# Output weights of attention B loaded at a later gate: the first piece of q of the fifth chunk in place of the fourth piece of q of the third

## The chip, the cores and the metric

The kernel runs on one core of a Trainium2 chip. The metric is the device time of one execution in microseconds; the median of several runs is compared. The core has a matmul engine (TensorE, PE in the profile, PEld for its weight loads), VectorE (DVE), ScalarE (ACT), GpSimd (POOL) and SyncE (SP). SyncE issues nearly all transfers between DRAM and on-chip memory, in order, on one hardware queue that sixteen DMA engines serve.

## The reference, cut to what matters

Two attentions over 2048 positions of width 640, with 32 heads of 20, side by side in the output. All inputs are bf16.

```python
def _A_ref(x, wq, wk, wv, wo, beta):            # 4 segments of 512
    for s in range(N):
        logits = einsum('bhqd,bhkd->bhqk', qs, ks) * scale + mask      # causal in the segment
        a_dot  = einsum('bhqk,bhkd->bhqd', softmax(logits), vs)
        a_mem  = (phi(qs) @ M) / (phi(qs) @ z + 1e-06)                 # memory of earlier segments
        o      = g * a_mem + (1.0 - g) * a_dot                         # g = sigmoid(beta)
        M, z   = M + phi(ks)^T vs, z + sum(phi(ks))
    return o @ wo
def _B_ref(x, wqkv, wo):                        # causal, window of 256
    o = softmax(masked(q k^T * Dh ** -0.5)) v
    return o @ wo
return concatenate([A, B], axis=-1)
```

## The kernel before

The work is cut into eight chunks of 512 positions that alternate between the two attentions: A0, B0, A1, B1, A2, B2, A3, B3. In the code they are numbered from 0, so the "third chunk" is number 2 (A1) and the "fifth" is number 4 (A2). Each chunk passes through these stages: q and k projected in five pieces of 128 columns (`qk_job`, result copied from PSUM by VectorE at line 557), v projected in two halves of four tiles (`v_job`; the copy to vA at line 733 multiplies by 1 − g), scores in batches (line 814), their exponential on ScalarE (line 830), masks on GpSimd (line 869) and VectorE (line 847), probabilities times v (line 883, line 904 in the last chunk), a transpose and a normalisation (lines 949 to 1000), and the output projection with wo (`final_job`, copied out at line 1099).

Some data must change partitions between stages, and that goes through transfers on SyncE's queue. Three of the eight head groups of q and k are stored to a scratch in DRAM (line 509) and read back in another layout (line 517); phi(q) and phi(k) go the same way (lines 619, 626, 651, 646). In the A chunks, once the first half of v is written to vA, two transfers copy the lower 64 rows of vA to a tile vS (line 757); the second half of v, which writes the same tile vA, may be written only after the first of these copies has read it. In the B chunks the tiles vL, vU and vX are filled alike (line 783). Outputs go through a scratch and a transposing transfer (lines 1021 and 1040) before the projection. The inputs x of later chunks are loaded in three pieces when their buffer comes free (line 355).

The order of TensorE's work is written out by hand in the string `PLAN`. The kernel is emitted once by a planner, `Flow`, that keeps an estimated time for each engine and for the DMA queue. It decides at which point of the emitted program a transfer is issued, and with that the order on SyncE's queue, which is then fixed. The weights wait in a list `self.loads`; each has a gate (a time that is known only when some earlier piece of work has been emitted) and a due time counted from the gate. The front of the list is issued when its gate is known and either the planned queue is idle or the due time has come:

```python
        t = max(self.sp - 100.0, self.fabric - BACK)
        gate, _, due = self.loads[0]
        if gate:
            if gate() is None:
                return None
            return min(max(t, gate() - 400.0), gate() + due)
```

`load_w` adds a weight tile of [128, 2, 5, 320] as two transfers of 400 KB, one for each half of its columns (line 319), each into a tile of its own that nothing else uses. The tile wo_B serves the output projections of B0, B1, B2 and most of B3. A third load, wo_end, stands behind it in the list with a gate in the last chunk.

In the emitted program each transfer of SyncE takes the next of eight completion semaphores in turn, and does not start before the transfer eight places earlier has landed.

Of the kernel before, what the change touches and what calls it, by code (L numbers as in the profile page):

```python
# [267 lines left out]
class _K:  # L268
# [1034 lines left out]
    def body(self, xA, A_wq, A_wk, A_wv, A_wo, A_beta, xB, B_wqkv, B_wo, out2d):  # L1303
# [65 lines left out]
                                   None, 22000.0)  # L1369
        wo = {}  # L1370
        wo["A"] = self.load_w("wo_A", A_wo, self.known(0, "scored"), 6000.0)
        wo["B"] = self.load_w("wo_B", B_wo[0], self.known(2, "q", 3), 6000.0)

        wo["end"] = self.load_w("wo_end", B_wo[1], self.known(NC - 1, "q", KT - 1), 9000.0,
                                self.wt["wk_A"][:].rearrange("p m k c -> p (m k c)").rearrange(
# [336 lines left out]
```

## Time and profile before

| what | value |
|---|---|
| runs | 332.38, 332.24, 330.19 us; median 332.24 |
| profiled execution | 332.54 us, its span 330.7 us |
| granted clock of TensorE | 1.000 |
| TensorE, ScalarE, GpSimd, VectorE busy | 96%, 91%, 80%, 77% of the span |
| transfers | 47.45 MB, mean 143 GB/s |
| wo_B issued by SyncE | from 73.17 us, 2 transfers |
| first matmul that reads wo_B | 149.6 us |

Busy time of TensorE is modelled from the instructions, so 96% does not say that it runs at its peak. In the rows quoted below, a time in brackets at the end of a timeline row is how long the engine stood still before it, with what ended that. "SPq" rows are the issuing of transfers by SyncE, not the movement of data. In the table of waits the three numbers are total microseconds, number of times and the longest.

### The profile page before, as it was taken

Reading aid. Unit: us, or ns where it says so; the run is one execution under the profiler, and the core shown is the slowest. Engines: PE = TensorE matmul, PEld = TensorE weight load, DVE = VectorE, ACT = ScalarE, POOL = GpSimd, SP = SyncE. Lnnn points to the kernel's source line nnn. Section 1 sums busy time; section 2 is a strip of 40 time slices with the busy share of each in tenths; the row PEclk is TensorE's granted clock in tenths of the full one; section 3 lists DMA queues with packets and bytes.
Section 4 is the critical chain, followed back from the end, with each engine's and each line's share of the span. In section 5 each row is a group of like instructions: output and inputs, shape, how many; then the busy total and the mean of one; then the engine's idle time right before and its main releaser. Section 6 shows DMA issues by size and latency. Waiting matters only on the chain.

```text
span 330.7 us, 16968 instructions
## 1 busy us (share of the span) xinstructions
PE 316.4 (96%) x7195; PEld 176.2 (53%) x7195; DVE 255.8 (77%) x533; ACT 299.6 (91%) x333; POOL 265.4 (80%) x672
## 2 busy tenths in 40 slices
PE   7999999998999999999999999999999999999984
PEld 2454546555445455646653546456654445666652
DVE  6777767797977787999867897988777798876753
ACT  1979999998999998989999999899999999979962
POOL 8466679997759899976886999998975899989850
PEclk9999999999999999999999999999999999999999
DMA  7975945675589354165689146117868027397642
GB/s 210 388 250 135 194 138 108 150 193 159 135 214 217 67 115 132 22 141 147 138 216 174 33 86 157 50 32 154 147 181 186 14 54 185 107 233 159 109 127 80
DMA packets 76266, 47.45 MB, mean 143 GB/s; under 512 B 48382, under 2 KB 73182, under 8 KB 76190
## 3 DMA queue, kind: packets, MB, share of 16 engines
q1 hardware_dynamic: 75469, 45.71, 57.7%
q8 instruction: 56, 0.92, 1.2%
q10 hardware_dynamic: 720, 0.66, 0.7%
q14 instruction: 21, 0.16, 0.2%
HBM read 17.62 MB, written 16.96 MB: 105 GB/s over the span
## 4 chain that ended last, share of the span: by engine, by line
PE 36%; DVE 5%; ACT 3%; DMA 2%; POOL 2%; issue 1%; SPq 1%; ACTq 0%; DVEq 0%
PE m L935 19%; PE sc L814 7%; PE m L883 5%; ACT pt L830 3%; PE m L930 2%; DVE tt L949 2%; PE m L904 1%; DMA xT<-scr_o 1%; DVE pt L847 1%; DMA scr_o<-o 1%; POOL pt L869 1%; DVE kA L557 1%; POOL o L987 1%; DVE ot L1099 0%; PE m L686 0%
## 5 line engine op out<-in xcount | busy, mean ns | idle before, releaser
L830 ACT ACTIVATE pt<-sc 128x1024 bf16<-128x1024 f32 (+2 forms) x306 | 282.9, 1026 | 15.1 <-PE sc L814 12.9
L869 POOL TENSOR_SCALAR_AFFINE_SELECT pt<-pt 128x128 bf16<-128x128 bf16 (+1 forms) x512 | 178.0, 376 | 49.8 <-ACT pt L830 42.8
L949 DVE STREAM_TRANSPOSE tt<-m 128x512 f32<-128x512 f32 x88 | 61.2, 709 | 24.7 <-PE m L883 15.9
L987 POOL TENSOR_TENSOR o<-tt,rr 128x320 bf16<-128x320 f32 x64 | 48.5, 758 | 4.7 <-DVE rr L977 3.9
L814 PE MATMUL sc<-qB,kB 20*64 20x64 bf16 (+2 forms) x1728 | 39.9, 217 | 0.8 <-ACT pt L830 0.3
L935 PEld LDWEIGHTS <-xT 128*128 128x128 bf16 x296 | 26.7, 97 | 18.4 <-issue 6.1
L847 DVE TENSOR_TENSOR pt<-pt,ends 128x1024 bf16<-128x1024 bf16 (+2 forms) x50 | 36.4, 739 | 0.0
L1099 DVE CAST ot<-m 128x320 bf16<-128x320 f32 x58 | 28.1, 486 | 9.8 <-PE m L935 8.4
L814 PEld LDWEIGHTS <-kB 20*64 20x64 bf16 (+1 forms) x1728 | 22.2, 98 | 22.4 <-issue 20.5
L814 PE MATMUL sc<-qA,kA 20*64 20x64 bf16 (+4 forms) x1024 | 33.5, 237 | 0.5 <-ACT pt L830 0.4
L935 PEld LDWEIGHTS <-oT 128*128 128x128 bf16 x244 | 21.5, 97 | 12.5 <-issue 3.3
L814 PEld LDWEIGHTS <-kA 20*128 20x128 bf16 (+1 forms) x1024 | 13.4, 97 | 22.4 <-issue 21.3
L935 PE MATMUL m<-wBv,xT 128*128 128x320 bf16 x147 | 24.2, 299 | 0.9 <-DVE tt L949 0.4
L883 PE MATMUL m<-pt,vA 128*32 128x192 bf16 (+3 forms) x512 | 23.6, 274 | 0.2
L935 PE MATMUL m<-wo_A,oT 128*128 128x320 bf16 x125 | 21.0, 300 | 0.8 <-DVE kA L557 0.8
L935 PE MATMUL m<-xT,wBq 128*128 128x512 bf16 x82 | 21.4, 380 | 0.3 <-DVE tt L949 0.3
L935 PE MATMUL m<-xT,wBk 128*128 128x512 bf16 x81 | 20.7, 381 | 0.0
L935 PE MATMUL m<-wv_A,xT 128*128 128x320 bf16 x119 | 20.0, 300 | 0.2 <-DVE vA L733 0.2
L738 DVE CAST vB<-m 128x320 bf16<-128x320 f32 x32 | 15.6, 488 | 5.4 <-PE m L935 3.1
L935 PE MATMUL m<-wo_B,oT 128*128 128x320 bf16 x109 | 18.6, 300 | 0.8 <-DVE tt L949 0.4
L557 DVE CAST qB<-m 128x512 bf16<-128x512 f32 x20 | 13.8, 688 | 6.7 <-PE m L930 3.4
L935 PE MATMUL m<-xT,wk_A 128*128 128x512 bf16 x69 | 17.7, 379 | 1.2 <-DMA xT<-in_A_x_dram 1.1
(127 smaller groups left out, 460.2 us busy)
## 6 DMA issues: line engine op xcount, KB each, us to landing
out_dram<-ot SPq DMA_DIRECT2D x29, 160.0 KB
scr_o<-o SPq DMA_DIRECT2D x28, 160.0 KB
xT<-in_B_x_dram SPq DMA_DIRECT2D x8, 288.0 KB
xT<-in_A_x_dram SPq DMA_DIRECT2D x8, 256.0 KB
scr_pk<-e SPq DMA_DIRECT2D x15, 128.0 KB
vS<-vA SPq DMA_DIRECT2D x16, 87.0 KB
vL<-vB SPq DMA_DIRECT2D x8, 174.0 KB
scr_kA<-kA SPq DMA_DIRECT2D x16, 60.0 KB
```

Source lines behind the costliest of these rows:

```text
L557: nc.vector.tensor_copy(out=dst[:, m, at:at + L], in_=ps[:, :])
L738: nc.vector.tensor_copy(out=dst, in_=src)
L814: nc.tensor.matmul(ps[j // 2][h0:h1, j % 2, c0:c0 + nq], lhsT=k[rows, g, k0:k0 + h1 - h0], rhs=q[rows, g, q0:q0 + nq], start=True, stop=Tr ...
L830: nc.scalar.activation(out=pt[:, :, lo:hi], in_=ps[i][:, :, lo:hi], func=ACT.Exp, scale=self.scale)
L847: nc.vector.tensor_tensor(out=blk, in0=blk, in1=self.ends[:, c0, :].unsqueeze(1).unsqueeze(1) .to_broadcast([P, 2, n // SH, SH]), op=ALU.mult)
L869: nc.gpsimd.affine_select(out=blk, in_=blk, pattern=pat, compare_op=ALU.is_ge, fill=self.zero, base=base, channel_multiplier=mul)
L883: nc.tensor.matmul(O[HD * j:HD * j + HD, q0:q0 + nq], lhsT=v[:, at_head(h):at_head(h) + HD], rhs=pts[j // 2][:, j % 2, c0:c0 + nq], start= ...
L930: self.nc.tensor.matmul(ps[s, 0:n], lhsT=lhsT[:, s], rhs=rhs, start=start, stop=stop, tile_position=(0, HD * j), skip_group_check=True)
L935: self.nc.tensor.matmul(ps[:, 0:n], lhsT=lhsT, rhs=rhs, start=start, stop=stop, skip_group_check=True)
L949: self.nc.vector.transpose(out=tt[:], in_=O[:, :])
L987: nc.gpsimd.tensor_tensor(out=to[:] if add_to else to, in0=a, in1=b, op=ALU.mult)
L1099: nc.vector.tensor_copy(out=ot[:, 320 * hf:320 * hf + 320], in_=ps[:, 0:320])
```

## The change

The gate of the load of wo_B is changed. It was the time at which piece 3 of q of chunk 2 is in SBUF; it is now that of piece 0 of q of chunk 4. Both halves, their size, their destination and their due times stay. In the emitted program the two transfers then stand on SyncE's queue behind the last piece of x for chunk 5 (line 355) and ahead of the stores of the output of chunk 3 (line 1021), where before they stood behind two stores of phi(k) of chunk 2 (line 651) and ahead of the copies to vS of chunk 2 (line 757).

```diff
-        wo["B"] = self.load_w("wo_B", B_wo[0], self.known(2, "q", 3), 6000.0)
+        wo["B"] = self.load_w("wo_B", B_wo[0], self.known(4, "q", 0), 6000.0)
```

## The prediction

> **What bounds the kernel now.** I read the page first: the busy shares, then the slices.
>
> ```profile
> span 330.7 us, 16968 instructions
> PE 316.4 (96%) x7195; PEld 176.2 (53%) x7195; DVE 255.8 (77%) x533; ACT 299.6 (91%) x333; POOL 265.4 (80%) x672
> PEclk9999999999999999999999999999999999999999
> DMA  7975945675589354165689146117868027397642
> ```
>
> TensorE is the bound and ScalarE is close behind it; the clock is full throughout. The transfers are far from a bound over the whole span, but uneven: the DMA slices (8.27 us each) run from 1 to 9 tenths. So a moved load can only matter where TensorE or ScalarE stands still because of it. The second view is the table of windows, cut at 10 us, around the old and the new place of the load:
>
> ```profile
> 70.00:80.00 10.00, 9.05 (x217) 4.64 (x199) 7.73 (x17) 10.00 (x14) 7.44 (x17) 1.00 0.61 167
> 80.00:90.00 10.00, 8.95 (x218) 5.59 (x219) 9.43 (x24) 8.51 (x11) 7.27 (x16) 1.00 0.46 101
> 90.00:100.00 10.00, 9.70 (x216) 4.68 (x215) 7.53 (x15) 9.75 (x12) 6.45 (x20) 1.00 0.83 222
> ...
> 120.00:130.00 10.00, 9.92 (x233) 5.66 (x232) 7.73 (x19) 9.54 (x11) 9.67 (x27) 1.00 0.56 152
> 130.00:140.00 10.00, 9.83 (x275) 5.76 (x273) 9.14 (x19) 9.34 (x11) 9.84 (x18) 1.00 0.05 10
> ```
>
> The columns are PE, PEld, DVE, ACT, POOL, the clock, the DMA share and GB/s. Between 70 and 90 us TensorE stands still for 0.95 + 1.05 = 2.0 us, the worst stretch before the tail; between 120 and 140 us it loses 0.25 us, and from 130 to 140 us the DMA engines are all but empty. The third view, the table of waits of the whole run, names what happens at 80 us:
>
> ```profile
> PEld L935 <- issue: 20.3, 75, 1.4
> ...
> DVE vA L733 <- DMA vS<-vA: 1.5, 1, 1.5
> ...
> PE m L883 <- DVE vA L733: 1.0, 1, 1.0
> ```
>
> VectorE waits once for a transfer, the copy from vA to vS, and TensorE once waits 1.0 us behind that. The timelines of SyncE, VectorE, TensorE and ScalarE show who stands in front of whom:
>
> ```profile
> 73.17 2.07 SPq L319 DMA_DIRECT2D wo_B<-in_B_wo_dram  x2
> 75.33 1.33 SPq L757 DMA_DIRECT2D vS<-vA  x2
> 76.75 1.76 SPq L509 DMA_DIRECT2D scr_qA<-qA  x4
> 81.26 1.43 SPq L517 DMA_DIRECT2D qA<-scr_qA  x4
> ...
> 75.00 0.48 DVE L733 TENSOR_TENSOR vA<-m,omg 128x320 bf16<-128x320 f32 x1
> ...
> 79.51 0.49 DVE L733 TENSOR_TENSOR vA<-m,omg 128x320 bf16<-128x320 f32 x1 [1.49 <-DMA vS<-vA]
> 80.35 0.91 DVE L598 TENSOR_TENSOR pq<-pq,e 128x512 bf16<-128x512 bf16 x1
> 82.80 0.42 DVE L598 TENSOR_TENSOR pq<-pq,e 128x512 bf16<-128x512 bf16 x1
> ...
> 80.06 0.29 PE L883 MATMUL m<-pt,vX 128*32 128x256 bf16 x4 [1.01 <-DVE vA L733]
> 81.91 0.84 PE L935 MATMUL m<-wo_A,oT 128*128 128x320 bf16 x5 [0.47 <-DVE kA L557]
> 85.15 0.84 PE L935 MATMUL m<-wo_A,oT 128*128 128x320 bf16 x5 [0.36 <-DVE kA L557]
> ...
> 81.95 1.06 ACT L577 ACTIVATE e<-kA 128x1024 bf16<-128x1024 bf16 x1 [0.93 <-DVE kA L557]
> 87.42 5.61 ACT L830 ACTIVATE pt<-sc 128x1024 bf16<-128x1024 f32 x6 [0.50 <-PE sc L814]
> 101.01 26.27 ACT L830 ACTIVATE pt<-sc 128x1024 bf16<-128x1024 f32 x28 [0.29 <-PE sc L814]
> ```
>
> The two halves of wo_B are issued at 73.17 us, the two copies to vS right behind them at 75.33. The next half of v may not overwrite vA before the copy has read it, so the write of line 733 stands still until 79.51, 4.2 us after the copy's issue. Its PSUM bank comes free late, TensorE waits 1.01 us; VectorE is then behind with kA, and TensorE (0.47, 0.36) and ScalarE (0.93) wait for that.
>
> **What the change removes.** Instructions and their order on TensorE, VectorE, ScalarE and GpSimd are the same in both programs. On SyncE's queue the two loads of wo_B move back past 65 other transfers: from ahead of the vS copies to behind the last piece of x for the sixth chunk. Nothing is added.
>
> ```profile
> wo_B<-in_B_wo_dram SPq DMA_DIRECT2D x2, 400.0 KB
> ```
>
> SyncE's time: 2.07 us of issue leave the old place. The copies to vS gain nothing by that, since they need the v write that begins at 75.00 and runs 0.48 us; they are issued at 75.33 either way. What they gain is the 800 KB ahead of them on the same queue. How long is their transfer without it? From both sides. At best it ends before VectorE is there and the whole 1.49 us goes:
>
> ```profile
> L757 SPq DMA_DIRECT2D vS<-vA x16: 590/602/1435, 15.2 to 241.8; - x16
> ...
>   DVE vA L733: 1.5, 1
> ```
>
> The first row counts sixteen copies to vS, eight pairs; the second, from the same answer, is who waited for them: line 733 once, for this pair alone. At worst it is as slow as the four stores of qA issued next, which still hold the load's tail in front of them: their issue ends at 76.75 + 1.76 = 78.51 and the read that needs them starts at 81.26, 2.75 us later. The first vS copy's issue ends near 75.33 + 1.33/2 = 76.0, so it would land at 78.75 and VectorE would still wait 0.75 us, gaining 0.75. I take 1.4 us of the 1.49, near the best end, as seven pairs of eight cost nothing.
>
> What comes through: TensorE regains its 1.01 us, and then, with VectorE earlier by 1.4, most of the 0.47 us; ScalarE regains 0.93 and then up to 0.50 at 87.42, as TensorE's scores come earlier. That makes 1.0 (TensorE's own wait alone) to 1.43 us (ScalarE's two), and I take 1.3. From 101.01 ScalarE runs 26 us without a break, and TensorE is 99% busy at 120 to 130 us, so a lead of both engines is kept; the transfers there are started by them and move along. The stores of qA land earlier too, which is worth nothing: no engine of the first table waits for them.
>
> **What it adds at the new place.** Three rows say what lies there.
>
> ```profile
> 125.39 1.63 SPq L355 DMA_DIRECT2D xT<-in_B_x_dram  x2
> 138.68 0.87 SPq L1021 DMA_DIRECT2D scr_o<-o  x2
> L935 PE MATMUL m<-wo_B,oT x109: 296/299/310, 149.6 to 306.6; 128*128 128x320 bf16 x109
> ```
>
> SyncE's queue is empty from 127.02 to 138.68 us: the load is issued into that gap, waits for nothing, and no transfer stands behind it. At the old place all of it, with the copies behind it, was down 79.51 − 73.17 = 6.3 us after its first issue, so here by about 133.4, and its first matmul is at 149.6: 16 us to spare. Cost 0; if the cover were gone, each microsecond of lateness would be a microsecond of the output projection. The eight completion semaphores that SyncE's transfers take in turn shift by two for the 65; each transfer then waits for the one eight before it, which at both ends has long landed.
>
> What shares the DMA engines with the load there are fetches of instructions:
>
> ```profile
> q8 instruction: 2, 0.03, 1.4%
> q14 instruction: 1, 0.01, 0.3%
> ```
>
> These are the queues of the window 127 to 138 us: three fetches. TensorE's longest wait put down to its own issue is 1.4 us in the whole run (first row of the table of waits above), so this costs between 0 and 1.4 us. In the stretch 68 to 95 us, which holds the load at its old place, the same group is short:
>
> ```profile
> PEld L935 <- issue: 2.0, 8, 0.4
> ```
>
> I take 0, by this nearer row. The Trainium skill (DMA: Bandwidth & Descriptors, "Queues, rings and completion order") states that each DMA engine takes turns between queues and changes only after a whole packet, by which a large load makes a fetch beside it slower. By that the move would carry a delay from the old place to the new, and with the 1.4 us row as its price the sum would be 1.3 less 1.4, no gain.
>
> **The sum.** The profiled execution took 332.54 us, 1.84 beyond its span of 330.7; 332.54 − 1.3 = 331.24. It lies 0.30 above the median of 332.24, so the median's counterpart is 330.94; I say 331.0.
>
> **The rivals.**
>
> 1. *The copy stays slow or the lead is lost.* If the copy lands as late as the stores of qA, 0.75 us of VectorE's wait remain and less than half comes through; a later shared wait can take the rest. For: the stretch 90 to 100 us has a DMA share of 0.83. Against: TensorE lost only 0.30 us there. Time: 332.2 to 331.7.
> 2. *The fetches pay.* 332.24 − 1.3 + 1.4 = 332.3. For: fetches do fall there. Against: above.
> 3. *Slower: VectorE and GpSimd fall out of step.* From 79 us both run at another offset. VectorE's masks of line 847 are short or long by what GpSimd does beside them:
>
> ```profile
> L847 DVE TENSOR_TENSOR pt<-pt,ends x50: 415/683/1210, 15.0 to 317.4; 128x1024 bf16<-128x1024 bf16 x44, 128x768 bf16<-128x768 bf16 x4, 128x512 bf16<-128x512 bf16 x2
> 79.00:330.70 251.70, 28.81 (x38) 1.00 0.56 126
> ```
>
> After 79 us the 38 masks take 28.81 us, 0.758 each, 2.9 us more than 38 at the median of 0.683. Twice that excess, all on the path, is 332.24 − 1.3 + 2.9 = 333.8. It ends slower than before from three more long masks on (0.53 us each over the median). For: line 598 above shows 0.91 and 0.42 us for one form. Against: VectorE is 77% busy, and a long mask is mostly absorbed.
>
> 4. *Faster by more.* The same offset falls well: no long masks, 332.24 − 1.3 − 2.9 = 328.0.
> 5. *The change doesn't do it*: the load would have to be issued elsewhere; the order on the queue excludes that.
>
> **How the numbers follow.** Likeliest case 0.54, with its own range 330.2 to 331.9; rival 1 0.12; rival 2 0.04; rival 3 0.15; rival 4 0.15. The bound for a change is 1% of 332.24, 3.3 us, about what a measurement of this kernel can tell from no change: 328.9 and 335.6. Faster by over 1% is rival 4 and 0.03 of the likeliest, as the runs before alone spread over 2.2 us: 0.18. Slower by over 1% is the far end of rival 3, nine more long masks or something unseen: 0.10. Within 1%: 0.72. The range runs from 328.6, inside rival 4, to 333.8, the middle of rival 3, and leaves out less than 0.2.
>
> **What would show it.** In the profile after: no wait of line 733 for the vS copy, or one under 0.3 us; no 1.0 us wait of TensorE for line 733; ScalarE's row at 81.95 about 0.9 us earlier and its long unbroken stretch starting near 99.7; wo_B issued near 125.7 and TensorE's issue waits unchanged between 125 and 140 us; the first matmul with wo_B waiting for no DMA. I am wrong if VectorE still waits over 0.75 us for vS, if TensorE between 75 and 90 us is idle as long as before, or if the lead at 101 us is there but gone at the end.

## The result, and the profile after

| | before | after |
|---|---|---|
| median of 9 runs each | 332.41 us | 329.87 us |
| lowest to highest | 330.19 to 333.32 us | 329.26 to 331.48 us |
| profiled execution, its span | 332.54, 330.7 us | 330.22, 328.5 us |

The ratio is 0.9932, with a 95% interval of 0.9906 to 0.9958: the kernel became faster by 0.7%, or 2.3 us with some 0.9 us to either side. That is more than the 1.3 us forecast and within the 1% that was called no clear change. The time lies inside the stated range, but 0.3 us below the likeliest case's own range of 330.2 to 331.9.

First the head of the page after, then its windows around the two places of the load (PE, PEld, DVE, ACT, POOL, clock, DMA share, GB/s):

```profile
span 328.5 us, 16933 instructions
PE 313.9 (96%) x7160; PEld 176.4 (54%) x7195; DVE 255.4 (78%) x533; ACT 299.4 (91%) x333; POOL 265.2 (81%) x672
```

```profile
70.00:80.00 10.00, 9.50 (x243) 5.41 (x242) 9.31 (x21) 10.00 (x14) 8.51 (x18) 1.00 0.44 101
80.00:90.00 10.00, 9.78 (x205) 5.55 (x209) 8.55 (x22) 9.96 (x12) 7.83 (x19) 1.00 0.60 137
90.00:100.00 10.00, 9.61 (x238) 4.90 (x229) 7.61 (x14) 9.71 (x12) 6.73 (x22) 1.00 0.75 200
...
120.00:130.00 10.00, 9.82 (x213) 5.19 (x203) 7.53 (x15) 8.98 (x10) 9.84 (x23) 1.00 0.67 205
130.00:140.00 10.00, 9.47 (x275) 5.75 (x278) 9.76 (x21) 9.52 (x11) 9.84 (x21) 1.00 0.23 47
```

The work is the same (35 matmul records are missing after, so PE's busy time reads a little low). Between 70 and 90 us ScalarE was busy 18.51 us and is now 19.96 of 20; TensorE went from 18.00 to 19.28. In the table of waits "DVE vA L733 <- DMA vS<-vA" and "PE m L883 <- DVE vA L733" no longer occur. The timelines after, for SyncE, VectorE, TensorE, GpSimd and ScalarE, beside the rows shown of before:

```profile
71.26 1.67 SPq L651 DMA_DIRECT2D scr_pk<-e  x2
74.19 1.73 SPq L757 DMA_DIRECT2D vS<-vA  x2
76.35 2.10 SPq L509 DMA_DIRECT2D scr_qA<-qA  x4
...
73.69 0.48 DVE L733 TENSOR_TENSOR vA<-m,omg 128x320 bf16<-128x320 f32 x1
...
74.82 0.48 DVE L733 TENSOR_TENSOR vA<-m,omg 128x320 bf16<-128x320 f32 x1
...
77.39 0.45 DVE L598 TENSOR_TENSOR pq<-pq,e 128x512 bf16<-128x512 bf16 x1
77.77 0.48 DVE L733 TENSOR_TENSOR vA<-m,omg 128x320 bf16<-128x320 f32 x1
...
78.67 0.42 DVE L598 TENSOR_TENSOR pq<-pq,e 128x512 bf16<-128x512 bf16 x1
...
79.01 0.68 DVE L557 CAST kA<-m 128x512 bf16<-128x512 f32 x1
...
78.70 0.28 PE L883 MATMUL m<-pt,vX 128*32 128x256 bf16 x4
...
79.97 0.69 PE L814 MATMUL sc<-qB,kB 20*64 20x64 bf16 x62 [0.40 <-ACT pt L830]
...
78.77 0.91 POOL L987 TENSOR_TENSOR o<-tt,rr 128x320 bf16<-128x320 f32 x1
...
74.18 1.08 ACT L577 ACTIVATE e<-qA 128x1024 bf16<-128x1024 bf16 x1
...
78.83 2.01 ACT L830 ACTIVATE pt<-sc 128x1024 bf16<-128x1024 f32 x2
80.64 1.14 ACT L577 ACTIVATE e<-kA 128x1024 bf16<-128x1024 bf16 x1
81.59 3.50 ACT L830 ACTIVATE pt<-sc 128x1024 bf16<-128x1024 f32 x4
84.97 0.63 ACT L577 ACTIVATE e<-kA 128x512 bf16<-128x512 bf16 x1
85.64 13.00 ACT L830 ACTIVATE pt<-sc 128x1024 bf16<-128x1024 f32 x14
98.93 26.27 ACT L830 ACTIVATE pt<-sc 128x1024 bf16<-128x1024 f32 x28 [0.29 <-PE sc L814]
```

The write of line 733 that stood until 79.51 now starts at 77.77 with no gap before it, and the vS copy is issued at 74.19 instead of 75.33. ScalarE, which stopped three times before, runs from 74 to 98.6 us with no gap in its timeline, and TensorE now waits once, 0.40 us, for ScalarE. Before, ScalarE stopped ahead of its rows at 81.95 and 87.42 us, as shown in the prediction, and a third time. That row of before, the one with which the stage begins, and two rows of VectorE and GpSimd behind the stall that are used below:

```profile
74.36 1.08 ACT L577 ACTIVATE e<-qA 128x1024 bf16<-128x1024 bf16 x1
...
93.28 7.44 ACT L830 ACTIVATE pt<-sc 128x1024 bf16<-128x1024 f32 x8 [0.25 <-PE sc L814]
...
81.18 0.68 DVE L557 CAST kA<-m 128x512 bf16<-128x512 f32 x1
...
80.25 0.73 POOL L987 TENSOR_TENSOR o<-tt,rr 128x320 bf16<-128x320 f32 x1 [1.32 <-DVE rr L977]
```

From this e<-qA row to the start of the stretch of 28 activations (101.01 before, 98.93 after; both behind a gap of 0.29 us) is a stage that contains the stall and nothing of the new place. It lasted 101.01 − 74.36 = 26.65 us before and 98.93 − 74.18 = 24.75 us after: 1.90 us shorter. This stage length is the measure for the experiments, since it doesn't mix with what varies elsewhere in a run.

The profiled spans differ by 2.2 us. At e<-qA the run after already led by 0.18 us; the stage makes that 2.08, and at the tail of the run 1.90 of it is left. What remains comes in the tail itself. Two rows of the chain that ended last belong to it, the store of the last outputs and the transposing read behind it. They follow for the kernel before, the one after, and experiment e2, which keeps the load at its old place:

```profile
308.12 3.23 DMA scr_o<-o
311.50 4.13 DMA xT<-scr_o
```

```profile
306.22 2.78 DMA scr_o<-o
309.14 4.26 DMA xT<-scr_o
```

```profile
306.84 2.87 DMA scr_o<-o
309.83 4.32 DMA xT<-scr_o
```

The first transfer was 0.45 us longer in the profiled run before than in the one after. But e2 has 2.87 us without the move, and two kernels without the stall, e3 and e6 below, have 3.12 and 3.32 us: that piece is a difference between executions, not of the change.

### The profile page after: what moved, and what is told of

It reads as the page before. It is cut to its first block, busy times and chain, and to the rows that moved or that the text cites. A ratio compares the mean times of both kernels' runs of the same rounds, so it can differ in the third digit from the quotient of the medians.

```text
span 328.5 us, 16933 instructions
## 1 busy us (share of the span) xinstructions
PE 313.9 (96%) x7160; PEld 176.4 (54%) x7195; DVE 255.4 (78%) x533; ACT 299.4 (91%) x333; POOL 265.2 (81%) x672
## 4 chain that ended last, share of the span: by engine, by line
PE 37%; DVE 4%; ACT 3%; DMA 2%; POOL 2%; issue 2%; SPq 0%; ACTq 0%; DVEq 0%
PE m L935 20%; PE sc L814 7%; PE m L883 5%; PE m L930 3%; ACT pt L830 3%; DVE tt L949 2%; DMA xT<-scr_o 1%; PE m L904 1%; POOL pt L869 1%; DMA scr_o<-o 1%; DVE pt L847 1%; POOL o L987 1%; DVE ot L1099 0%; PE m L686 0%; PE sc L935 0%
## 5 line engine op out<-in xcount | busy, mean ns | idle before, releaser
L949 DVE STREAM_TRANSPOSE tt<-m 128x512 f32<-128x512 f32 x88 | 61.2, 709 | 24.7 <-PE m L883 15.8
L883 PE MATMUL m<-pt,vA 128*32 128x192 bf16 (+3 forms) x512 | 23.6, 274 | 0.2
L935 PE MATMUL m<-xT,wBq 128*128 128x512 bf16 x73 | 20.6, 380 | 0.8 <-DVE tt L949 0.3
L935 PE MATMUL m<-xT,wBk 128*128 128x512 bf16 x70 | 19.6, 380 | 0.7 <-issue 0.3
L557 DVE CAST kB<-m 128x512 bf16<-128x512 f32 x20 | 13.6, 681 | 6.6 <-PE m L935 5.8
```

What stands on the lines that cost most here:

```text
L557: nc.vector.tensor_copy(out=dst[:, m, at:at + L], in_=ps[:, :])
L883: nc.tensor.matmul(O[HD * j:HD * j + HD, q0:q0 + nq], lhsT=v[:, at_head(h):at_head(h) + HD], rhs=pts[j // 2][:, j % 2, c0:c0 + nq], start= ...
L935: self.nc.tensor.matmul(ps[:, 0:n], lhsT=lhsT, rhs=rhs, start=start, stop=stop, skip_group_check=True)
L949: self.nc.vector.transpose(out=tt[:], in_=O[:, :])
```

## The experiments

The theory (A): the wait of VectorE for the vS copy, which stood behind the load, is the whole gain. The rivals: (B) emptier DMA engines from 73 to 82 us help all transfers; the new place itself brings or costs something; and, from the prediction, engines that fall out of step. The stage length in the table is taken in each kernel from the same two ScalarE rows as above. Each ratio is against runs of the kernel before on the same chip, whose medians were 332.29 us for e1, e2, e4 and e5 and 332.45 us for e3, e6 and e7. One column comes from the traces' semaphore events: each transfer ends with increments of its completion semaphore, sixteen for a vS copy or a half of wo_B (one record is missing in e4), and the last of them is taken as its landing. The column gives the time from the start of the issue of the first vS copy to its landing.

| kernel | load of wo_B | median | ratio to before, 95% interval | stage 74 to 100 us | first vS copy, issue to landing | wait of line 733 for vS |
|---|---|---|---|---|---|---|
| before | ahead of vS | 332.41 | 1 | 26.65 | 4.09 | 1.49 |
| after | at 123 us | 329.87 | 0.9932 (0.9906 to 0.9958) | 24.75 | 2.24 | none |
| e1_behind | right behind vS | 330.37 | 0.9936 (0.9904 to 0.9968) | 24.90 | 2.40 | none |
| e2_one_issue | ahead of vS, one transfer | 332.55 | 1.0015 (0.9981 to 1.0049) | 26.22 | 4.76 | 1.20 |
| e3_one_half | one half ahead of vS | 330.51 | 0.9933 (0.9908 to 0.9959) | 24.74 | 3.38 | none |
| e4_no_load | none | 330.27 | 0.9949 (0.9921 to 0.9978) | 24.74 | 2.23 | none |
| e5_twice | at both places | 331.89 | 0.9987 (0.9960 to 1.0013) | 26.73 | 4.72 | 1.77 |
| e6_two_tiles | ahead of vS, vA in two tiles | 330.20 | 0.9931 (0.9884 to 0.9978) | 24.75 | 4.82 | none |
| e7_chunk_on | at 141.6 us | 330.21 | 0.9927 (0.9893 to 0.9961) | 24.74 | 2.50 | none |

**e1_behind.** The parts of the load are taken from the list and issued in `v_squares` after the copies of chunk 2, first half.

```diff
+            if n == 2 and half == 0:
+                for _, part, _ in self.behind:
+                    part()
```

> The load of wo_B stays in its old stretch but stands behind the two vS copies of the third chunk instead of ahead of them; all else as before. Theory A (the gain is the wait of VectorE for the vS copy and nothing else): the wait of line 733 is gone, ratio to before 0.992 to 0.996, about 330 us. Rival B (the gain is the emptier DMA engines from 73 to 82 us, for all transfers there): the 800 KB are still there, ahead of the stores of qA, so at most a third of the gain, 0.998 or above.

SyncE's and VectorE's timelines of this run:

```profile
73.96 1.73 SPq L757 DMA_DIRECT2D vS<-vA  x2
75.74 1.07 SPq L319 DMA_DIRECT2D wo_B<-in_B_wo_dram  x2
76.91 1.90 SPq L509 DMA_DIRECT2D scr_qA<-qA  x4
...
77.53 0.48 DVE L733 TENSOR_TENSOR vA<-m,omg 128x320 bf16<-128x320 f32 x1
```

Two places on the queue give the gain. The 800 KB still cross the DMA engines in the same stretch, ahead of the stores of qA (the first lands at 80.88 us here, at 78.70 in the kernel after), and cost at most 0.15 us of stage: rival B falls. "All else as before" does not hold quite: in this kernel alone the planner also put eight other transfers earlier on the queue, four stores of phi(q), two later vS copies with a store of phi(k), and one transposing read. The copies to vU that follow it begin at 109.32 us, against 104.57 after, and a write of vB waits 0.76 us for such a copy at 115.85, in no other kernel. This profiled run lost about a microsecond late, 0.48 us of it between 98.84 and 126.06, around that wait; the runs' median does not show it. With its order unchanged, e6 is the cleaner test of rival B.

**e2_one_issue.** Same place, same 800 KB, one transfer.

```diff
+            nc.sync.dma_start(out=wob[:], in_=B_wo[0])
+        self.loads.append((self.known(2, "q", 3), whole_load, 6000.0))
```

> The load stays at its old place but as one transfer of 800 KB in place of two of 400 KB. It shows what of the delay of vS is SyncE's time for the issue and what is the bytes ahead on the queue. If the bytes decide: the vS copy is issued about 1 us earlier, near 74.3 us, but lands as late, the wait of line 733 stays at 1.2 to 1.5 us, ratio 0.998 to 1.001. If the issue time decides: the wait shrinks to 0.5 us or less, ratio 0.994 to 0.997.

```profile
72.62 0.42 SPq L1375 DMA_DIRECT2D wo_B<-in_B_wo_dram  x1
73.83 1.73 SPq L757 DMA_DIRECT2D vS<-vA  x2
...
78.69 0.49 DVE L733 TENSOR_TENSOR vA<-m,omg 128x320 bf16<-128x320 f32 x1 [1.20 <-DMA vS<-vA]
```

SyncE is free after 0.42 us instead of 2.07, so the copies are issued as early in the stage as in the kernel after, yet VectorE still waits 1.20 us of 1.49 and the stage gains 0.43 of 1.90. The copy lands 4.76 us after its issue, against 2.24 after: most of the delay is the bytes ahead on the queue. Whether the earlier issue is worth the other 0.29 us is not shown, since e5 below, with two loads ahead like before, differs from before by as much the other way (1.77 against 1.49). The ratio is a hair above the 0.998 to 1.001 expected, with 1.000 inside its interval.

**e3_one_half.** One half stays ahead of the copies, the other gets the new gate.

```diff
+        _, part1, due1 = self.loads.pop()
+        self.loads.append((self.known(4, "q", 0), part1, due1))
```

> The first half of wo_B stays at the old place, the second half moves to the new one. SyncE then needs about 0.45 us for the issue and is ready for the vS copy in time; 400 KB stand ahead of it. If the bytes decide the delay in proportion, the vS copy lands about 2 us earlier and the wait of line 733 is 0 to 0.3 us, ratio 0.993 to 0.996. If any load ahead of the copies keeps the wait, 0.997 to 1.000.

```profile
72.61 0.42 SPq L319 DMA_DIRECT2D wo_B<-in_B_wo_dram  x1
73.82 1.73 SPq L757 DMA_DIRECT2D vS<-vA  x2
...
77.39 0.48 DVE L733 TENSOR_TENSOR vA<-m,omg 128x320 bf16<-128x320 f32 x1
```

The issue rows are those of e2 to 0.01 us; only the bytes differ, 400 KB against 800. With 400 the wait is gone and the stage is at its full gain: the second 400 KB are what made the copy late enough to matter. It is a narrow escape: the copy lands at 77.20 us, 0.19 us ahead of the write.

**e4_no_load.** wo_B isn't loaded; the output projection of attention B uses wo_A's tile, with the same matmuls.

```diff
+        wo["B"] = wo["A"]
```

> As the changed kernel, but wo_B is not loaded at all; the output projection of attention B multiplies by wo_A in its place, the same matmuls. It prices the new place: theory A expects the changed kernel's time, 0.992 to 0.995 of before, that is a cost of the new place of 0 to 0.3 us. If the load disturbs fetches or other transfers at its new place, this is faster than the changed kernel by 0.5 us or more, below 0.991.

The stage equals that of the kernel after, and the median is not below it: the load costs nothing measurable at its new place. (The profiled execution of this kernel took 333.24 us at a mean granted clock of 0.993, 0.96 behind 280 us, so its rows are read for the stage only.)

**e5_twice.** The old place and the new one both load the same data.

```diff
+        self.load_w("wo_B", B_wo[0], self.known(4, "q", 0), 6000.0, wo["B"])
```

> wo_B is loaded at the old place and once more, the same data, at the new place. Theory A: the old stall is back in full and the new place is free, ratio 0.999 to 1.001. If the new place itself brings something (the order of completion semaphores, the offset of VectorE against GpSimd), 0.995 to 0.998; if it costs, above 1.002.

```profile
72.69 1.71 SPq L319 DMA_DIRECT2D wo_B<-in_B_wo_dram  x2
74.50 1.32 SPq L757 DMA_DIRECT2D vS<-vA  x2
...
79.31 0.49 DVE L733 TENSOR_TENSOR vA<-m,omg 128x320 bf16<-128x320 f32 x1 [1.77 <-DMA vS<-vA]
```

The stall is back in full, the ratio's interval holds 1.000 (the ratio itself is just below the 0.999 expected), and 800 KB more at the new place do not show. Removing the old place is the change; the new one is only where the load does no harm.

**e6_two_tiles.** The load stays; vA becomes two tiles, so the second half of v has nothing to wait for.

```diff
-        self.vA = self.v_tile("vA")
+        halves = [big.tile([P, LT, HV], BF16, name="vA%s" % x) for x in "xy"]
+        self.vA = Halves(halves)          # picks the tile by the column
```

> The load stays as before; vA is made of two tiles, one for each half of its columns, so that the second half of v has nothing to wait for. Theory A: the late vS copy holds up nobody, the wait of line 733 is gone, ratio 0.992 to 0.996 with the load at its old place. Rival B: the load still fills the DMA engines there, 0.998 or above.

```profile
73.34 2.11 SPq L331 DMA_DIRECT2D wo_B<-in_B_wo_dram  x2
75.55 1.33 SPq L769 DMA_DIRECT2D vS<-vAx  x2
...
78.12 0.48 DVE L745 TENSOR_TENSOR vAy<-m,omg 128x320 bf16<-128x320 f32 x1
```

(Lines are shifted by 12; L745 is line 733.) The order on the queue is the same as before, the first copy lands at 80.37 us, 2.2 us behind the start of this write, and the gain is whole: 24.75 us. The late copy cost time only through the one write that waited for it. The two halves of v don't overlap in their columns, so that wait was for the tile, not for data.

**e7_chunk_on.** The gate is `known(4, "q", 3)`.

> The gate of the load is the fourth piece of q of the fifth chunk; the load then stands on the queue behind the vS copies of the fifth chunk. Theory A: the gain at 79 us is there as in the changed kernel, about 2 us; but the load is issued near 141 us and lands near 146 to 148, when the first matmul with it is due (147.6 us in the changed kernel). TensorE waits for it 0 to 2 us: ratio 0.993 to 0.999. It prices a load that comes too late.

The timeline of SyncE and the answer on the tile wo_B:

```profile
141.58 1.33 SPq L319 DMA_DIRECT2D wo_B<-in_B_wo_dram  x2
...
L935 PE MATMUL m<-wo_B,oT x109: 296/299/310, 147.9 to 304.9; 128*128 128x320 bf16 x109
```

The load is issued 6.3 us ahead of its first matmul, and its halves land at 145.06 and 146.92 us, the second 1.0 us ahead of it. The matmul waits for no DMA; the 0 of "0 to 2 us" was the outcome, and the ratio is just below the 0.993 expected. The price of a load that comes too late was not reached by this run.

No kernel stands apart from the one after: five ways to remove the same wait end between 0.9927 and 0.9949, their intervals overlapping.

## Why the prediction was right or wrong

**Right: the place and the chain.** Line 733 waits for vS because of the load ahead, TensorE and ScalarE wait behind it; all of it vanished, and e1, e5 and e6 show it from three sides.

**Right: VectorE's wait, and the side chosen.** 1.4 of 1.49 us was taken; all 1.49 went. The slower end, the copy landing as late as the stores of qA with 0.75 us left, was not approached: it landed 2.24 us after its issue.

**Wrong: "the copies to vS gain nothing by" SyncE's time.** The first copy reads tiles 0 and 2 of v and needs only the third write of line 733 (73.69 us after), not the fourth that begins at 75.00. It was held by the issue of the load: 75.33 before, 74.19 after, 0.96 us earlier once the 0.18 us is taken off. The sum did not suffer, since it let nearly the whole wait go by the bytes alone. No run tried them alone; as an estimate, the 2.24 us of the kernel after behind the old issue at 75.33 would end at 77.57, ahead of VectorE, which began to wait at 79.51 − 1.49 = 78.02.

**Mis-sized: "what comes through", 1.3 us with 1.43 as the upper bound.** The stage gave 1.90. The bound counted two gaps of ScalarE, 0.93 + 0.50, as the whole loss. Taken from start to start, the first costs more than its gap: from the row of line 830 ahead of it to e<-kA are 81.95 − 79.01 = 2.94 us before and 80.64 − 78.83 = 1.81 after, 1.13 less, because rows that do not wait overlap (e<-kA after starts at 80.64 although its predecessor ends at 78.83 + 2.01 = 80.84). The next step, to 87.42 before and 85.64 after, is worth 0.47. The rest, to the stretch of 28, is worth 0.30; the third gap of 0.25 at 93.28 lies there, in a row that was not quoted. The third gap is no fixed part of the stall: e2 and e5 do not have it, and there the same three parts are 0.84, 0.47, 0.16 and 1.41, 0.47, 0.10.

The 1.13 can be traced. The cast to kA that e<-kA reads starts at 81.18 before and 79.01 after, 1.99 us earlier once the 0.18 us is taken off. That is the wait of 1.49 and 0.5 more, since VectorE's operation of line 598 behind the stall takes 0.91 us before and 0.42 at 78.67 after. Of the 1.99, ScalarE had 0.86 to spare. In e2 and e5 the same sum holds to 0.01 us: 1.20 and 1.77 of wait, 0.5 of line 598, less 0.86. So the prediction had the chain right and took its gaps for the loss; that it saw VectorE earlier by 1.4 and not by 1.99 us cost it nothing, since it counted ScalarE's gap of 0.93 whole.

Two of its readings are loose, without effect on the sum: the DMA slices run from 0 and not from 1 tenth, and TensorE stood still as long, 2.03 us, in the first 10 us of the run.

**Right: the lead is kept.** ScalarE's later long stretch began 2.08 us earlier at 98.93 (near 99.7 was forecast), and the store of the last outputs still 1.90 us earlier, at 306.22. The tables of waits from 121 to 137 us after, and from 123 to 139 us before, have the same rows for TensorE's issue:

```profile
PEld L814 <- issue: 2.0, 6, 0.4
PEld L930 <- issue: 0.6, 3, 0.2
```

The table after has one new row of VectorE, 0.90 us for the copy to vU, ahead of line 557 at 123.50. It is no cost of the new place: before, the same gap of 0.90 us stood there and was put down to TensorE, and e4 has it without any load. The rival of the fetches (332.3 us) did not occur, and the Trainium skill's rule on taking turns between queues (DMA: Bandwidth & Descriptors, "Queues, rings and completion order") changes nothing that this trace shows: the load was in flight from 123.45 to 128.89 us with two fetches beside it, and no wait for issue is longer than before.

**Rivals 3 and 4, engines out of step, did not occur where they were priced.** After 77 us the 38 masks of line 847 take 28.79 us, against 28.81 after 79 us before:

```profile
77.00:327.00 250.00, 28.79 (x38) 1.00 0.58 131
```

Their mechanism did act on one operation, the one of line 598 above. Where the stall stands, GpSimd's operation of line 987 waits for VectorE and starts 0.10 us ahead of it: line 598 takes 0.91 us and line 987 0.73. Without the stall, line 987 starts 0.10 us behind it: 0.42 and 0.91. Line 598 took 0.91 us in all three kernels with the stall and 0.42 or 0.43 in the six others. That the one engine slows the other there is argued from this pattern; no run separates them.

**The sum against the median.** Stage 1.90 us as measured in one profile, ratio 2.3 ± 0.9 us: they agree. Forecast 331.0, measured 329.87; the missing 1.1 us are 0.6 us of stage (1.90 less 1.3) and a rest of 0.5 us inside the interval of the ratio, for which no cause was shown.

## What to carry to other kernels

A bulk load can have a price at its place on a queue that no bandwidth share shows: look for the small transfer issued right behind it and for who waits for that. Moving the load behind the small transfer, halving what stands ahead, or giving the waiting writer its own tile all paid the same here; halving did so with 0.2 us to spare. Size such a gain on the engine that sets the pace behind the stall, here ScalarE. Measure from start to start of its rows and not by its gaps, and follow the operand it waits for: how late it comes, with every operation on the way that runs longer, less what the engine had to spare.

## What the runs showed of the hardware that was not expected

With the issue alike, the first vS copy took 2.24 us to land with nothing ahead of it on the queue (after), 3.38 with 400 KB (e3) and 4.76 with 800 KB (e2): about 1.1 and 1.4 us for each 400 KB. VectorE needs the copy some 3.6 us after its issue (77.39 − 73.82 in e3), so only the third made it wait. With 800 KB ahead the time spread from 4.09 to 4.82 us over four kernels. In e2 fifteen of the sixteen increments had come by 77.67 us and the last came at 78.59, so 0.9 us of its wait hung on one of them; the cause is open.

Two transfers of 400 KB held SyncE 2.07 us (before) and 1.71 us (e5), one of 800 KB 0.42 us (e2). It is not the size: one of 400 KB took 0.42 us too (e3), and where two follow each other one of them took 0.37 to 0.43 us and the other 0.59 to 1.63. Why is open. And the executions are nearly exact copies of each other where nothing disturbs them: the stage of 24.7 us came out at 24.74 or 24.75 us in five different kernels.
